# Block-sparse attention and a GELU feed-forward on one core: where the second batch's V is asked for, where GpSimd's copies stand, and how the last product is laid out

## The chip, the cores and the metric

The kernel runs on one core of one Trainium2 chip. The metric is the device time of one execution in microseconds (us); the figure for a kernel is the median of several runs. Engines are named as in the profile: PE (TensorE, matrix products, with PEld for its weight loads), DVE (VectorE), ACT (ScalarE), POOL (GpSimd) and SP (SyncE). Each works through its own list of instructions in order and waits at an instruction until what it needs is there.

## The reference

Attention over 4 batches, 8 heads, 768 positions and 64 numbers a head, in blocks of 32 positions. A query block sees its neighbours, the first and the last block and three sampled ones; the first and the last query block see everything. A feed-forward layer with exact GELU follows, on 3072 tokens.

```python
scores = scale * np.matmul(q, k.transpose(0, 1, 3, 2))
mask = np.abs(blk_i - blk_j) <= window
mask = mask | (blk_i == 0) | (blk_j == 0) | (blk_i == n_blocks - 1) | (blk_j == n_blocks - 1)
for qb in range(n_blocks):
    for kb in sampled_blocks[qb]:
        mask[qb * block:(qb + 1) * block, kb * block:(kb + 1) * block] = True
attn = softmax(np.where(mask, scores, -1e9))      # shortened
x = matmul(attn, v), heads side by side           # 3072 x 512
h = x @ w_in                                      # 512 x 2048
out = (0.5 * h * (1.0 + erf(h * inv_sqrt2))) @ w_out
```

## The kernel before, in words

The 24 tiles of 128 tokens ("quads") are cut into nine **units**: three for batch 0 (one, two and three quads) and two for each further batch (three quads each). Unit numbers run from 0 to 8. A unit goes through attention, then FFN1 (the product with `w_in` and GELU, into the buffer `g`), then FFN2 (the product with `w_out`). The order of instructions on each engine is the order in which the code is written. The loop at the end of the kernel takes unit n: it issues FFN1 of n (`ffn1_step`, eight steps with a GELU each), then attention of unit n+1, into which FFN2 of unit n is strewn as **pieces**. A piece is one matrix product `op` of 128x512; 16 of them make one quad, so a unit has 16, 32 or 48. After the sixteenth, ACT copies the result out of the accumulator (`os`), and SP stores it. There is one accumulator bank for `op`, so the next quad's first piece waits for that copy.

`attention(unit, filler, quota, tail)` goes round by round: PE's scores (`sc`), DVE's maxima (`nm`), ACT's exponentials (`pp`), DVE's transposes (`pT`, `ptd`), PE's products with V (`av`), DVE's division (`den`, `rec`, `xh`), PE's output transposes (`tx`) and ACT's copy into `xT`, which FFN1 reads. `quota` says how many pieces stand in each round, the first number belonging to the round before the first exponentials; `tail` says how many stand ahead of the last `av` group and how many ahead of the last output transposes. What is left over is written behind those transposes.

A round of one unit is "dense" (first and last query block, all keys) or sparse (up to two query blocks). Units 0, 3, 5 and 7 have four dense rounds. I call the transitions into units 3, 5 and 7 **fresh**, since a new batch begins there: its K and Q heads are turned during FFN1 of units 2, 4 and 6. The transitions into units 4, 6 and 8 are **plain**.

Sampled blocks: `gather` copies the keys and values of the sampled blocks of K|V (`kv`, two buffers, one for even and one for odd batches) into `gb`, one copy a block, by DVE or, for the last four query blocks of unit 1, by POOL. The DVE copies for a fresh unit (33 in one go) stand in the second FFN1 step and read the V of that batch. V is loaded by POOL's DMA queue, eight loads a batch, one a head (`load_v`). `hold_loads` puts a one-element copy of `g` ahead of loads on POOL, so that they go out only after a given GELU. The queue is shared with `kn`, `qn` (the next batch's K and Q), `w_in` and `w_out`.

The last unit's FFN2 has no attention beside it.

Of the kernel before, what the change touches and what calls it, by code (L numbers as in the profile page):

```python
# [9 lines left out]
F32 = mybir.dt.float32  # L10
# [9 lines left out]
def kernel(  # L20
# [11 lines left out]
    P = 128  # L32
# [402 lines left out]

    def ffn2_pieces(n):
        for t, quad in enumerate(units[n].quads):
            op = psO.tile([P, D_MODEL], F32, name="op")
            for m in range(KOUT):
                nc.tensor.matmul(op, lhsT=g[:, m, t * P:(t + 1) * P], rhs=w_out_sb[:, m, :],  # L440
                                 start=(m == 0), stop=(m == KOUT - 1))
                if m != KOUT - 1:
                    yield
            os = opool.tile([P, D_MODEL], F32, name="os")
            nc.scalar.copy(os, op)  # L445
            row = units[n].b * S + quad * P
            nc.sync.dma_start(out=out[row:row + P, :], in_=os)
            yield

# [64 lines left out]
    for part in range(2):  # L514
# [3 lines left out]
    gather(units[1], J0[7:], others, KC, BW, nc.gpsimd)  # L518
    ones(1)
    attention(units[0], iter(()), [0] * 7, (0, 0), 5,  # L520
              {4: [lambda: gather(units[0], units[0].js, known, KC, BW)],
               5: [lambda: nc.scalar.copy(kvs[0][:, :, 0:KC], k0)]})

    QUOTAS = {0: ([0, 2, 4, 4, 2], (2, 2)), 1: ([4, 4, 4, 4, 3, 3, 1], (2, 7))}
    for n, unit in enumerate(units):
# [4 lines left out]
        if nxt is not None and not fresh:  # L530
# [4 lines left out]
            elif n == 1:  # L535
                known |= block_numbers(J1[:6], DVE)
                gather(nxt, J1[:4], known)
                hooks[-1] = [lambda u=nxt: gather(u, J1[4:6], known)]
# [6 lines left out]
        for s in range(KOUT // 2):  # L545
            ffn1_step(n, 2 * s)
            if s == 0:
                if n > 0 and not fresh and b + 1 < B:
                    hold_loads(0)
                    for hs in HALVES:  # L550
                        load_kq(kn, k, b + 1, hs)
                    for hs in HALVES:
                        load_kq(qn, q, b + 1, hs)
                if fresh and (b == 0 or b + 2 < B):
                    hold_loads(0)
                    if b == 0:
                        for h in range(H):
                            load_v(1, h)
                    if b + 2 < B:
                        for h in range(H):  # L560
                            load_v(b + 2, h)
# [18 lines left out]
        if nxt is None:  # L580
            for _ in filler:
                pass
        elif n in QUOTAS:
            attention(nxt, filler, *QUOTAS[n], hooks=hooks)
        elif fresh:
            attention(nxt, filler, [4] * 8 + [1, 1, 0], (3, 11))
        else:
            attention(nxt, filler, [6, 5, 5, 5, 5, 6, 2], (3, 11))
# [30 lines left out]
```

## Time and profile before

| | |
|---|---|
| median of 3 runs | 342.42 us (341.29 to 343.58) |
| the profiled execution | 344.02 us, of which the span of the trace is 342.2 |
| PE matmul / weight load busy | 272.3 us (80%) / 155.3 us (45%) |
| DVE busy | 222.0 us (65%) |
| ACT busy | 218.6 us (64%) |
| POOL busy | 51.6 us (15%) |
| chain that ended last, shares of the span | PE 50%, DVE 17%, ACT 15%, DMA 7%, issue 6%, POOL 3% |

Busy shares are means over the whole span. The chain follows the work that ended last back through what released it; "issue" there is time in which an engine waited for nothing that the profile shows. The time between span and run (1.8 us) lies outside the trace.

### The profile page before, as it was taken

How to read it: one execution, taken by the hardware profiler on the slowest of the kernel's cores; microseconds unless marked ns; L12 is line 12 of the kernel's file. 1: busy time of each engine (PE TensorE's matmuls, PEld its weight loads, DVE VectorE, ACT ScalarE, POOL GpSimd, SP SyncE). 2: the span in 40 equal slices, each digit the busy share in tenths (PEclk: the TensorE clock that was granted, in tenths of full speed). 3: DMA queues.
4: the chain of work that ended last, by engine and by line, in shares of the span. 5: the costliest groups of instructions: out<-in, count | busy, mean ns of one | idle time of the engine just before them, and what ended most of it. 6: DMA issues, size and time to landing. Idle time of an engine off the chain costs nothing.

```text
span 342.2 us, 12767 instructions
## 1 busy us (share of the span) xinstructions
PE 272.3 (80%) x5608; PEld 155.3 (45%) x5608; DVE 222.0 (65%) x553; ACT 218.6 (64%) x377; POOL 51.6 (15%) x98
## 2 busy tenths in 40 slices
PE   1753877867991876989899878988898878997994
PEld 1522735534650353535554445545553445454541
DVE  6598666794619795758298887485498877582000
ACT  8675486865482684588367883795378765884621
POOL 8674001100760000300060001200000000000000
PEclk9999999989997899999999999999999999999999
DMA  7999900910999000571099001911000000001001
GB/s 117 134 141 206 178 2 34 179 41 4 86 80 53 33 34 4 100 117 63 35 75 21 33 34 35 173 46 35 33 1 33 33 6 33 1 34 62 3 31 63
DMA packets 39193, 20.74 MB, mean 61 GB/s; under 512 B 25825, under 2 KB 36066, under 8 KB 39138
## 3 DMA queue, kind: packets, MB, share of 16 engines
q0 software_dynamic: 35680, 13.63, 62.9%
q1 hardware_dynamic: 3458, 6.29, 4.8%
q8 instruction: 44, 0.72, 1.0%
q14 instruction: 11, 0.09, 0.1%
HBM read 27.26 MB, written 6.29 MB: 98 GB/s over the span
## 4 chain that ended last, share of the span: by engine, by line
PE 50%; DVE 17%; ACT 15%; DMA 7%; issue 6%; POOL 3%; DVEq 1%; ACTq 0%; POOLq 0%
PE hp L432 22%; PE op L440 14%; ACT pp L324 8%; PE av L387 7%; DVE nm L312 5%; DMA kv<-in_v_dram 4%; DVE pT L341 3%; DMA w_in_sb<-in_moe_w_in_dram 3%; PE sc L287 3%; DVE gb L251 3%; ACT L351 2%; ACT os L445 2%; DVE xh L404 2%; POOL kv L107 2%; ACT g L434 2%
## 5 line engine op out<-in xcount | busy, mean ns | idle before, releaser
L324 ACT ACTIVATE pp<-sc,nm 128x256 bf16<-128x256 f32 (+1 forms) x192 | 91.1, 592 | 21.1 <-DVE nm L315 10.5
L440 PE MATMUL op<-w_out_sb,g 128*128 128x512 bf16 x384 | 97.4, 385 | 5.3 <-ACT os L445 3.3
L432 PE MATMUL hp<-xT,w_in_sb 128*128 128x384 bf16 (+2 forms) x576 | 90.6, 316 | 7.7 <-ACT xT L419 7.7
L434 ACT ACTIVATE g<-hp 128x768 bf16<-128x768 f32 (+2 forms) x72 | 53.3, 740 | 46.1 <-PE hp L432 46.0
L432 PEld LDWEIGHTS <-w_in_sb 128*128 128x128 bf16 x576 | 54.8, 102 | 36.5 <-issue 8.8
L312 DVE TENSOR_REDUCE nm<-sc 128x4 f32<-128x1024 f32 (+1 forms) x48 | 53.1, 1108 | 14.8 <-PE sc L287 14.7
L251 DVE COPY gb<-kv 128x388 bf16 (+1 forms) x252 | 49.6, 277 | 16.0 <-issue 7.4
L440 PEld LDWEIGHTS <-g 128*128 128x128 bf16 x384 | 33.1, 98 | 47.3 <-issue 17.0
L387 PE MATMUL av<-kv,pT 64*32 64x130 bf16 x1760 | 33.4, 229 | 13.6 <-DVE xh L404 7.7
L387 PEld LDWEIGHTS <-pT 64*32 64x32 bf16 x2816 | 28.8, 94 | 23.6 <-DVE xh L404 11.5
L341 DVE STREAM_TRANSPOSE pT<-pp 128x512 f32<-128x512 f32 (+1 forms) x48 | 31.5, 657 | 6.9 <-ACT pp L324 6.8
L287 PEld LDWEIGHTS <-qT 64*32 64x32 bf16 x832 | 10.6, 90 | 50.8 <-issue 41.2
L445 ACT COPY os<-op 128x512 f32<-128x512 f32 x24 | 14.1, 587 | 28.5 <-PE op L440 28.1
L287 PE MATMUL sc<-gb,qT 64*32 64x256 bf16 x704 | 19.6, 283 | 15.9 <-ACT pp L324 15.8
L124 POOL COPY mark<-g 1x1 bf16<-1x1 bf16 x5 | 2.1, 418 | 154.0 <-ACT g L434 154.0
L107 POOL DMA_DIRECT2D kv<-in_v_dram x32 | 23.4, 737 | 4.9 <-DMA kv<-in_v_dram 2.2
L419 ACT COPY xT<-tx 128x512 bf16<-128x512 bf16 (+1 forms) x24 | 13.5, 562 | 16.4 <-PE tx L414 16.4
L387 PE MATMUL av<-gb,pT 64*32 64x130 bf16 x1056 | 20.9, 230 | 2.0 <-issue 2.0
L351 ACT ACT_TABLE_LOAD x17 | 21.8, 1283 | 0.3
L400 DVE TENSOR_SCALAR den<-av 128x8 f32<-128x8 f32 (+2 forms) x28 | 4.3, 155 | 23.6 <-PE av L387 23.1
L404 DVE TENSOR_TENSOR xh<-av,rec 128x512 bf16<-128x512 f32 (+2 forms) x28 | 18.3, 652 | 1.0
L315 DVE TENSOR_REDUCE nm<-sc 128x1 f32<-128x768 f32 x16 | 15.2, 955 | 3.2 <-PE sc L287 3.2
(58 smaller groups left out, 194.3 us busy)
## 6 DMA issues: line engine op xcount, KB each, us to landing
out_dram<-os SPq DMA_DIRECT2D x24, 256.0 KB, 2.0
kn<-in_k_dram POOLq DMA_DIRECT2D x8, 384.0 KB, 5.4
qn<-in_q_dram POOLq DMA_DIRECT2D x8, 384.0 KB, 8.0
kv<-in_v_dram POOLq DMA_DIRECT2D x32, 96.0 KB, 7.7
w_in_sb<-in_moe_w_in_dram POOLq DMA_DIRECT2D x4, 512.0 KB, 12.9
w_out_sb<-in_moe_w_out_dram POOLq DMA_DIRECT2D x2, 1024.0 KB, 20.6
raw<-in_sampled_blocks_dram SPq DMA_DIRECT2D x1, 0.6 KB
```

The source lines that it names most:

```text
L107: nc.gpsimd.dma_start(out=kvs[b % 2][32 * hh:32 * hh + 32, 0:NB, c0:c0 + D], in_=v[b, h].rearrange("(n p) d -> p n d", p=BL))
L251: (engine or nc.vector).tensor_copy(sampled(unit.place[j], r)[:, None, c0:c1], src[:, bass.ds(at[j][r], 1), :])
L287: nc.tensor.matmul(o, lhsT=qT[rows, pr, BL * j:BL * j + BL], rhs=rhs(rows, pr), start=True, stop=True)
L312: nc.vector.tensor_reduce(out=nm[:, 0:2 * n].rearrange("p (g j) -> p g j", g=2), in_=A4[:, :, 0:n, :], op=ALU.max, axis=AX.X, negate=True)
L324: nc.scalar.activation(dst.rearrange("p (c k e) -> p c e k", e=2, k=BL), src.rearrange("p (c e k) -> p c e k", e=2, k=BL), AF.Exp, bias=bias)
L341: nc.vector.transpose(pt[:, 0:w].bitcast(F32), pp[:, 0:w].bitcast(F32))
L351: nc.scalar.activation(junk, zero[0:1, 0:1], func)
L387: nc.tensor.matmul(av[32 * s:32 * s + 32, h, V2 * G:V2 * G + V2], lhsT=pv[rows, c // 2, :, c % 2], rhs=src[rows], start=(c == 0), stop=(c ...
L404: nc.vector.tensor_tensor(xh[rows, :, 0:m * D].rearrange("p h (x d) -> p h x d", d=D), a[:, :, :, 0:D], rec[rows, :, 0:m, None].to_broadca ...
L432: nc.tensor.matmul(hp[:, i, 0:T], lhsT=w_in_sb[:, ki, (m + i) * P:(m + i + 1) * P], rhs=xTs[n % 2][:, ki, 0:T], start=(ki == 0), stop=(ki ...
L434: nc.scalar.activation(g[:, m:m + 2, 0:T], hp[:, :, 0:T], AF.Gelu)
L440: nc.tensor.matmul(op, lhsT=g[:, m, t * P:(t + 1) * P], rhs=w_out_sb[:, m, :], start=(m == 0), stop=(m == KOUT - 1))
```

## The change

There are five edits. V of batch 1 is asked for in the first step of unit 0's FFN1 instead of unit 2's, behind its own `hold_loads(0)`. POOL's twelve value copies for unit 1 (and the ones that complete `kv` 1) stand behind DVE's value copies for unit 0, held by a one-element copy from the block that DVE writes last. In FFN1 of unit 1, DVE makes all eighteen first copies for unit 2 ahead of attention, where six stood behind the first maxima. The numbers of pieces in each round and tail are others: more in the early rounds, fewer ahead of the last transposes, two or three behind them. The last unit's FFN2 goes to four accumulator areas, its last quad in two halves of 256 columns.

```diff
+    def last_output(n):
+        jobs = [(t, quad, slice(0, D_MODEL)) for t, quad in enumerate(units[n].quads)]
+        t, quad, cols = jobs.pop()
+        jobs += [(t, quad, slice(D_MODEL * i // 2, D_MODEL * (i + 1) // 2)) for i in range(2)]
+        two = psV.tile([P, 2, D_MODEL], F32, name="av", tag="V")
+        banks = [psO.tile([P, D_MODEL], F32, name="op"), two[:, 0, :], two[:, 1, :],
+                 psT.tile([P, D_MODEL], F32, name="op", tag="T")]
+        for (t, quad, cols), bank in zip(jobs, banks):
+            op = bank[:, 0:cols.stop - cols.start]
+            for m in range(KOUT):
+                nc.tensor.matmul(op, lhsT=g[:, m, t * P:(t + 1) * P], rhs=w_out_sb[:, m, cols],
+                                 start=(m == 0), stop=(m == KOUT - 1))
+            store(n, quad, cols, op)
...
-    gather(units[1], J0[7:], others, KC, BW, nc.gpsimd)
-    ones(1)
+    def second_values():
+        nc.gpsimd.tensor_copy(mark, sampled(units[0].place[units[0].js[-1]], NR - 1)[0:1, BW - 1:BW])
+        gather(units[1], J0[7:], others, KC, BW, nc.gpsimd)
+        ones(1)
...
-               5: [lambda: nc.scalar.copy(kvs[0][:, :, 0:KC], k0)]})
-    QUOTAS = {0: ([0, 2, 4, 4, 2], (2, 2)), 1: ([4, 4, 4, 4, 3, 3, 1], (2, 7))}
+               5: [lambda: nc.scalar.copy(kvs[0][:, :, 0:KC], k0), second_values]})
+    QUOTAS = {0: ([0, 2, 4, 4, 1], (1, 2)), 1: ([6, 5, 5, 4, 3, 2, 2], (1, 2))}
...
-                gather(nxt, J1[:4], known)
-                hooks[-1] = [lambda u=nxt: gather(u, J1[4:6], known)]
+                gather(nxt, J1[:6], known)
...
+                if n == 0:
+                    hold_loads(0)
+                    for h in range(H):
+                        load_v(1, h)
...
-                if fresh and (b == 0 or b + 2 < B):
+                if fresh and b + 2 < B:
                     hold_loads(0)
-                    if b == 0:
-                        for h in range(H):
-                            load_v(1, h)
...
-            for _ in filler:
-                pass
+            last_output(n)
...
-            attention(nxt, filler, [4] * 8 + [1, 1, 0], (3, 11))
+            attention(nxt, filler, [5, 5, 6, 4, 4, 4, 4, 2, 2, 2, 0], (2, 5))
-            attention(nxt, filler, [6, 5, 5, 5, 5, 6, 2], (3, 11))
+            attention(nxt, filler, [8, 8, 5, 5, 6, 2, 2], (3, 6))
```

How POOL's list changes in the loop, as a difference from before (-) to now (+); `kv_86` and `kv_87` are the buffers of the even and the odd batches, and `mark` is the one-element copy that holds the loads.

```order
 L129 MEMSET kv_87 32x24x2 x4
 L124 COPY mark<-g 1x1
+L107 DMA kv_87<-in_v_dram 32x24x64 x8
+L124 COPY mark<-g 1x1
 L101 DMA kn<-in_k_dram 96x4x512 x2
 L101 DMA qn<-in_q_dram 96x4x512 x2
 L124 COPY mark<-g 1x1
-L107 DMA kv_87<-in_v_dram 32x24x64 x8
 L107 DMA kv_86<-in_v_dram 32x24x64 x8
```

The eight loads of batch 1's V moved ahead of K and Q of that batch, so that only batch 2's eight are left where sixteen stood.

ACT's list in the fresh transition from unit 2 to unit 3, from the table load for exponentials on; the 128x12x2x32 form of `pp` is a dense round, four of the other form are a sparse one.

```order
 L351 ACTIVATE junk<-zero 1x1
-L324 ACTIVATE pp<-sc,nm 128x12x2x32 x3
-L445 COPY os<-op 128x512
-L324 ACTIVATE pp<-sc,nm 128x12x2x32
-L324 ACTIVATE pp<-sc,nm 128x4x2x32 x10
-L445 COPY os<-op 128x512
+L324 ACTIVATE pp<-sc,nm 128x12x2x32 x2
+L439 COPY os<-op 128x512
+L324 ACTIVATE pp<-sc,nm 128x12x2x32 x2
+L324 ACTIVATE pp<-sc,nm 128x4x2x32 x6
+L439 COPY os<-op 128x512
+L324 ACTIVATE pp<-sc,nm 128x4x2x32 x4
```

The first two copies `os` moved ahead of one dense and of one sparse group of exponentials.

ACT's list at the end of the same transition, where FFN1 of unit 3 begins with the first `g`.

```order
-L419 COPY xT_95<-tx 128x4x128
-L445 COPY os<-op 128x512
-L419 COPY xT_95<-tx 128x4x128
+L419 COPY xT_95<-tx 128x4x128 x2
+L439 COPY os<-op 128x512
 L434 ACTIVATE g<-hp 128x768 x8
```

The third `os` moved behind the last copy into `xT`.

## Rows read from the trace of the kernel before

**Rows 1.** Chain that ended last: start, us, what. FFN1 of units 2 to 7.

```profile
85.60 1.47 PE hp L432 x8
...
137.06 10.57 PE hp L432 x64
...
168.42 1.46 PE hp L432 x8
...
209.79 10.57 PE hp L432 x64
...
241.75 1.46 PE hp L432 x8
...
283.89 10.57 PE hp L432 x64
```

**Rows 2.** Timeline of DVE, 101 to 110 us: start, us, what, idle before.

```profile
102.22 5.93 DVE L251 COPY gb<-kv 128x388 bf16 x33 [6.85 <-DMA kv<-in_v_dram]
108.06 1.82 DVE L315 TENSOR_REDUCE nm<-sc 128x1 f32<-128x768 f32 x2
```

**Rows 3.** The same chain, two stretches in unit 3's attention.

```profile
127.55 1.96 issue
...
131.51 1.45 issue
```

**Rows 4.** Windows from the start into each of these stretches; (x) counts instructions.

```profile
0.00:128.50 128.50, 87.64 (x2010) 54.27 (x2010) 90.28 (x222) 83.90 (x140) 38.70 (x79) 0.96 1.30 88
0.00:132.50 132.50, 89.64 (x2138) 55.60 (x2138) 91.50 (x223) 86.06 (x143) 38.70 (x79) 0.96 1.26 85
```

**Rows 5.** Timeline, 24 to 36 us, copies of POOL, DVE and ACT.

```profile
24.28 4.22 POOL L251 COPY gb<-kv 128x260 bf16 x12
24.92 5.71 DVE L251 COPY gb<-kv 128x260 bf16 x12
...
30.71 2.86 ACT L522 COPY kv<-qT 128x3200 bf16<-128x3200 bf16 x1 [3.89 <-DVE gb L251]
...
35.66 0.61 DVE L235 COPY gb<-qT 128x768 bf16<-128x768 bf16 x2
```

**Rows 6.** The chain again: DVE's value copies of unit 0.

```profile
28.50 2.13 DVE gb L251 x11
```

**Rows 7.** All instructions on the tile w_out_sb.

```profile
L118 POOL DMA_DIRECT2D w_out_sb<-in_moe_w_out_dram x2: 876/881/886, 18.9 to 20.2; - x2
...
DMA to landing us min/median/max: 18.7/20.6/22.5
```

**Rows 8.** Timeline, 280 to 284 us: end of unit 7's attention.

```profile
280.19 2.54 PE L440 MATMUL op<-w_out_sb,g 128*128 128x512 bf16 x11
...
280.51 0.69 DVE L404 TENSOR_TENSOR xh<-av,rec 128x512 bf16<-128x512 f32 x1
...
282.56 0.39 PE L414 MATMUL tx<-identity,xh 128*128 128x128 bf16 x4
...
282.76 0.59 ACT L445 COPY os<-op 128x512 f32<-128x512 f32 x1 [1.79 <-PE op L440]
...
283.24 0.59 ACT L419 COPY xT<-tx 128x512 bf16<-128x512 bf16 x1
```

**Rows 9.** Timeline of ACT, 188 to 190.5 us: dense rounds of unit 5.

```profile
188.25 1.11 ACT L324 ACTIVATE pp<-sc,nm 128x768 bf16<-128x768 f32 x1 [0.65 <-DVE nm L315]
189.62 0.59 ACT L445 COPY os<-op 128x512 f32<-128x512 f32 x1 [0.26 <-PE op L440]
```

**Rows 10.** Timeline, unit 2's first round on DVE.

```profile
65.44 1.10 DVE L251 COPY gb<-kv 128x388 bf16 x6
```

**Rows 11.** Timeline: FFN1 of unit 1, and the last product.

```profile
56.74 7.15 PE L432 MATMUL hp<-xT,w_in_sb 128*128 128x256 bf16 x64 [0.67 <-ACT xT L419]
...
334.48 3.61 PE L440 MATMUL op<-w_out_sb,g 128*128 128x512 bf16 x16 [0.72 <-ACT os L445]
...
338.18 0.59 ACT L445 COPY os<-op 128x512 f32<-128x512 f32 x1 [3.74 <-PE op L440]
```

More of the change, by code (lines that the diff above doesn't have):

```diff
@@ L434, in ffn1_step, with store @@
         nc.scalar.activation(g[:, m:m + 2, 0:T], hp[:, :, 0:T], AF.Gelu)
+    def store(n, quad, cols, op):
+        w = cols.stop - cols.start
+        os = opool.tile([P, w], F32, name="os")
+        nc.scalar.copy(os, op)
+        row = units[n].b * S + quad * P
+        nc.sync.dma_start(out=out[row:row + P, cols], in_=os)
     def ffn2_pieces(n):
@@ L443, in ffn2_pieces @@
                     yield
[L444 to L447, printed above, removed]
+            store(n, quad, slice(0, D_MODEL), op)
             yield
+    def last_output(n):
[11 more added lines that the diff above has]
+            store(n, quad, cols, op)
     def attention(unit, filler, quota, tail, held=0, hooks=None):
@@ L553 @@
                         load_kq(qn, q, b + 1, hs)
-                if fresh and (b == 0 or b + 2 < B):
+                if fresh and b + 2 < B:
                     hold_loads(0)
-                    if b == 0:
-                        for h in range(H):
-                            load_v(1, h)
-                    if b + 2 < B:
-                        for h in range(H):
-                            load_v(b + 2, h)
+                    for h in range(H):
+                        load_v(b + 2, h)
                 if fresh:
```

## The prediction

> **What bounds the kernel now.** I began with the chain that ended last, to find the places where FFN1 starts: they cut the run into stages that can be compared with each other [rows 1]. From one FFN1 start to the next, a stage with a fresh transition takes 137.06 - 85.60 = 51.46 us the first time, 209.79 - 168.42 = 41.37 the second and 283.89 - 241.75 = 42.14 the third. All three do the same work, so some 9.3 to 10.1 us of the first are waits. The timeline shows the largest: DVE stands 6.85 us until V of batch 1 has landed, then makes its 33 copies in 5.93 us, and only at 108.06 comes to the first maxima [rows 2]. Late in the same stage PE stands 1.96 and 1.45 us for nothing that the profile names [rows 3]. The counts up to these stops are 2010 and 2138 matmuls with as many weight loads [rows 4]: 128 pairs, 256 instructions apart. PE goes on at 129.51 and 132.96, 3.45 us apart. I read this as the supply of PE's instructions, in portions of 256, of which one takes some 3.45 us to come; a stretch of short products with V uses them up faster. Elsewhere the kernel is bound by a relay of PE, DVE and ACT inside attention, by PE in FFN1, and at the end by PE and ACT taking turns.
>
> **V of batch 1.** Nothing is added or removed in work, eight loads move from behind 85.60 to about 36 us (an estimate: the first GELU of unit 0, moved as below). Sixteen loads in a row landed in at most 102.22 - 85.60 = 16.6 us [rows 1, 2], so eight asked for at 36 are there long before DVE wants them; that wait goes whole. What is late next is known, since the second and third fresh stages have no such wait: the stage becomes 41.37 us [rows 1], if PE's instructions come in time. The first fresh stage begins at the same instruction count as before, since each stage keeps its number of pieces, so the borders between portions still fall into its products with V. Going through the new order with the durations of the second fresh stage and 3.45 us for a portion, I find PE at three borders early, by 1.0, 1.6 and 0.5 us; about 1.0 of this replaces waits that the stage has anyway, so I add 2.1. Gain: 51.46 - (41.37 + 2.1) = 8.0, and 0.1 from the pieces (below): 8.1 us. The ends: 10.1 if no portion is late, and 51.46 - 41.37 - 1.96 - 1.45 = 6.7 if both stops stay as they are.
>
> The moved loads pass POOL's queue. They stand behind `w_out`, whose second half is asked for at 20.2 and lands by 20.2 + 22.5 = 42.7 [rows 7]. On POOL only K and Q of batch 1 are queued behind them, held until the first GELU of unit 1's FFN1, which starts at 56.74 today [rows 11]. I cost the move at nothing, because they are queued after `w_out`; what it would cost if they shared the engines with it is a rival below.
>
> *A rule against this reading of PE's stops.* The Trainium skill ("Runtime: NRT & Kernel Launch", section "Instruction fetch mechanics") says that instructions come in blocks of 256, which agrees with rows 4, and that crossing from one to the next is mostly hidden, which rows 3 contradict at two places. By that rule the sum would keep the whole 10.1.
>
> **GpSimd's value copies.** POOL's twelve copies run from 24.28 to 28.50, DVE's twelve start at 24.92 [rows 5], and eleven of them run from 28.50 to 30.63 [rows 6]. So DVE's first copy sat through POOL's, and a copy takes 2.13 / 11 = 0.19. Alone the twelve end at 24.92 + 2.3 = 27.2 instead of 30.63: 3.4 us earlier, and unit 0's transposes, products, division and FFN1 follow DVE there. POOL's copies now wait for DVE and then for ACT's 2.86 us copy of the keys [rows 5], which starts near 27.2: they run from about 30.1 to 34.3. DVE reaches its fixed copies for unit 1 at 35.66 - 3.4 = 32.3 [rows 5] and would stand until 34.3, 2.0 us, if POOL again held it to the end. Those copies have a lead over unit 1's first scores of about the same size, as FFN1 of unit 0 lies between. I take 0.2 as the cost, and 0 to 2.0 as its bounds. Gain 3.2, between 1.4 and 3.5.
>
> *What the skill says of this.* "SBUF — State Buffer", section "SBUF: two separate sides", in the Trainium skill, calls the port that VectorE and GpSimd share a lock for one whole instruction. Rows 5 and 6 show more: DVE waited through all that was left of twelve instructions. By the page DVE would get in between two of them, and the 0.2 would be gone.
>
> **Unit 2's first round.** Six copies of 1.10 us stand between its first and second maxima [rows 10]. They move into FFN1 of unit 1, where DVE waits for scores. The exponentials follow the maxima there, so about 0.9 comes back. Here the third `os` no longer stands ahead of the last copy into `xT`, and PE has fewer pieces ahead of the last transposes, worth 0.7, against three pieces more ahead of the last product with V (0.2 each). Sum 1.3 us, between 0.5 and 1.8.
>
> **The pieces.** At the end of a stage `xh` is ready at 280.51 + 0.69 = 281.20, but eleven pieces last until 282.73, so the transposes run at 282.56; then `os` delays `xT` to 283.24 [rows 8]. With five pieces of 0.23 us ahead, PE is free at 281.35, `tx` runs then and `xT` starts at about 281.9: 1.3 us earlier. The three pieces left run beside the 0.59 us of `xT`, which nearly hides them. So a full transition returns 1.3. Against that, pieces moved ahead delay attention. In a fresh transition 5 + 5 + 6 pieces fill the first quad two groups of exponentials in, and its `os` stands ahead of the third, where before `os` came at 189.62, behind the exponentials of 188.25 [rows 9]. ACT must now wait for the longer run of pieces (to 188.5, as I walk it) and copy for 0.59: the third exponentials start at 189.1 or so, 0.9 later. Each round hands that on, since the accumulator of the scores is freed by the exponentials, and three more pieces, 0.7 us, stand in the rounds. Followed to the end, the last product with V ends 1.2 us later, of the gain of 1.3 there remains 0.1. In a plain transition two pieces more stand in the rounds and `os` moves one group earlier; followed through, that costs 0.3, and PE's stop at a portion border becomes 0.1 shorter, which leaves 1.1. Sum: three plain transitions 3.3, the two fresh ones not yet counted 0.2. Bounds: fresh from a loss of 1.0 to a gain of 1.3, plain from 0.1 to 1.3. The transition into unit 1 has 16 pieces, and its last transposes already wait for `xh`: nothing.
>
> **The last product.** Two times PE waits for `os`, 0.72 us each or nearly [rows 11]: 1.4, since each quad now has its own bank. Two halves cost no more than one whole: with 256 columns 64 products took 7.15, so 32 take 3.58, against 3.61 for 16 full ones. The last copy, 0.59, has half the columns, about 0.2 to 0.3 less, and its store half the bytes, 0 to 0.3. Sum 1.7, between 1.4 and 2.0.
>
> **Sum.** 8.1 + 3.2 + 1.3 + 3.3 + 0.2 + 1.7 = 17.8 us. The profiled execution took 344.02, 342.2 of it the span, so its like would take 326.2; against the median of 342.42, which is 1.6 lower, it is **324.6 us**.
>
> **The rivals.**
> *Instructions come in time.* The first fresh stage becomes like its twins, 41.37 us. For it: the second stage passes the same kind of products without a stop. Against it: rows 3 and 4, and that the borders lie where they lay. Then the gain is 19.8 to 20: 322.5 us.
> *The moved pieces eat what they free.* If every early piece delays the scores, and `os` the exponentials, by its whole length, a fresh transition loses 1.0 and a plain one gains nothing: 17.8 - 3 x 1.1 - 3.3 = 11.2, so 331.2 us. For it: ACT's idle time ahead of `os` in rows 9 is only 0.26 us. Against it: PE waits for exponentials in the same rounds, so part of a piece is free.
> *The loads hold up w_out.* Eight loads could share the engines with the second half of `w_out` and delay it by half of the 16.6 us above, 8.3; FFN2 of unit 0 wants it, by my walk, some 3 us after it lands today. Loss 5: 329.6 us. Against it: the loads are asked for 15 us later.
> *Slower than before: portions late everywhere.* Eight transitions hold products with V, and in the fresh ones two pieces instead of three stand between the last two groups of them. If each transition had two stops like rows 3, 3.41 us, of which 2.1 is already counted once, that would cost 8 x 3.41 - 2.1 = 25.2: 349.8 us. It outweighs the 17.8 from (17.8 + 2.1) / 8 = 2.5 us per transition on. Against it: the plain transitions keep five pieces there, and the fresh ones gain two ahead of the last group but one.
>
> **How the numbers follow.** Chances: the forecast 0.54 (322.9 to 328), instructions in time 0.24, moved pieces 0.14, loads against `w_out` 0.03, slower 0.02; and 0.03 that several losses together leave less than 1%, which is about what a measurement of this kernel tells from no change. The bounds of single terms do not add up to more than 4 us either way. A range of 320.5 to 330.5 leaves out the slow half of the piece rival and the last three, some 0.15. Faster by over 1%: 0.95; within 1%: 0.03; slower: 0.02.
>
> **What the profile after would show.** No wait of DVE for V ahead of unit 3, and first maxima some 7 us sooner behind the start of unit 2's FFN1 than the 108.06 - 85.60 = 22.5 of now. DVE's value copies of unit 0 done in 2.3 us. Transposes of the last group within 1.5 us of the last product with V, and `xT` straight behind. In fresh transitions an `os` ahead of the third exponentials and a last product with V about 1.2 us later than now. PE without a gap in the last product. The prediction is wrong if the first fresh stage still takes over 45 us, if fresh stages grow, or if FFN1 of unit 0 doesn't start some 3 us earlier.

## The result

The changed kernel takes 330.07 us (median of four runs, 329.59 to 330.38), the kernel before 343.00 in the same comparison: ratio 0.9625, interval 0.9579 to 0.9672. The profiled execution took 329.59 us with a span of 327.81, against 342.17 before: 14.36 us less, where the terms of the sum gave 17.8. In the timed runs the medians are 12.93 apart.

Stage by stage: "first" is the start of the first FFN1 in the timeline, "0" to "7" run from the first matmul of one unit's FFN1 to that of the next, "8" from the last FFN1 to the end. Stages 2, 4 and 6 hold the fresh transitions; 3, 5 and 7, the plain ones, are added up. All rows are of the one profiled execution of each kernel; the last column is the median of its timed runs, in us like all the others. The runs e1 to e12 are the experiments below.

| | first | 0 | 1 | 2 | 4 | 6 | 3+5+7 | 8 | span | median |
|---|---|---|---|---|---|---|---|---|---|---|
| before | 37.08 | 19.66 | 28.87 | 51.46 | 41.37 | 42.14 | 94.90 | 26.70 | 342.17 | 343.00 |
| after | 33.61 | 21.29 | 28.25 | 43.45 | 43.25 | 41.69 | 90.87 | 25.41 | 327.81 | 330.07 |
| e1 V late | 33.63 | 19.36 | 28.54 | 52.44 | 43.00 | 42.00 | 90.79 | 25.33 | 335.07 | 335.34 |
| e2 old pieces | 33.60 | 21.06 | 29.03 | 43.69 | 41.36 | 41.85 | 95.19 | 25.40 | 331.18 | 337.18 |
| e3 mixed pieces | 33.61 | 21.03 | 28.21 | 43.87 | 41.37 | 42.25 | 91.55 | 25.40 | 327.29 | 330.24 |
| e4 borders moved | 37.33 | 19.65 | 28.15 | 41.32 | 41.32 | 43.37 | 92.66 | 25.40 | 329.20 | 330.20 |
| e5 GpSimd first | 35.54 | 20.16 | 28.22 | 42.57 | 41.32 | 41.32 | 91.27 | 25.94 | 326.34 | 329.06 |
| e6 even fresh | 33.66 | 23.11 | 29.49 | 42.11 | 40.26 | 40.15 | 91.14 | 25.40 | 325.32 | 326.49 |
| e7 even, padded | 33.20 | 22.44 | 28.21 | 41.25 | 39.82 | 41.30 | 90.77 | 25.39 | 322.37 | 323.77 |
| e8 V alone | 37.13 | 20.22 | 28.66 | 43.09 | 41.36 | 41.84 | 94.63 | 26.70 | 333.64 | 335.75 |
| e9 V one FFN1 later | 33.61 | 19.64 | 30.77 | 42.13 | 41.30 | 41.31 | 91.25 | 25.32 | 325.33 | 327.09 |
| e10 = e6 and e9 | 33.29 | 20.05 | 29.94 | 42.57 | 39.79 | 39.89 | 90.23 | 25.32 | 321.09 | 322.97 |
| e11 = e10, padded | 33.61 | 19.93 | 29.67 | 40.70 | 39.82 | 39.82 | 90.82 | 25.32 | 319.70 | 321.08 |
| e12 changed, again | 33.21 | 21.11 | 28.44 | 45.01 | 41.32 | 41.96 | 91.08 | 25.40 | 327.53 | 329.32 |

The chain that ended last after the change, at the places of [rows 1 and 3]. Where the record of a first product is missing, it names an FFN1 up to 0.2 us late.

```profile
33.61 3.01 PE hp L432 x32
...
50.32 1.68 issue
...
54.90 7.18 PE hp L432 x64
...
83.15 1.46 PE hp L432 x8
...
118.47 1.19 issue
...
126.60 10.56 PE hp L432 x64
...
156.87 1.38 PE hp L432 x8
...
200.19 10.40 PE hp L432 x64
```

One of the two stops of PE in stage 2 (the lines "issue") is left, and there is a new one of 1.68 us in stage 0, where the chain before had none.

DVE's timeline in FFN1 of unit 2 answers [rows 2]:

```profile
92.74 5.71 DVE L251 COPY gb<-kv 128x388 bf16 x33
98.52 0.96 DVE L315 TENSOR_REDUCE nm<-sc 128x1 f32<-128x768 f32 x1
```

The wait for V is gone. The first maxima come 98.52 - 83.15 = 15.4 us behind the start of FFN1, 7.1 sooner.

The timeline from 24 to 36 us answers [rows 5 and 6]:

```profile
24.91 1.98 DVE L251 COPY gb<-kv 128x260 bf16 x12
...
26.93 2.86 ACT L545 COPY kv<-qT 128x3200 bf16<-128x3200 bf16 x1
...
29.85 4.33 POOL L251 COPY gb<-kv 128x260 bf16 x12 [2.71 <-ACT kv L545]
...
32.18 1.65 DVE L235 COPY gb<-qT 128x768 bf16<-128x768 bf16 x6
```

DVE's twelve copies take 1.98 us instead of 5.71. Its fixed copies for unit 1 run in 1.65 us in the middle of GpSimd's burst: the block of up to 2.0 us that the prediction kept as a bound did not come.

The end of unit 7's attention, timeline of PE, ACT and DVE, against [rows 8]:

```profile
269.92 0.69 DVE L404 TENSOR_TENSOR xh<-av,rec 128x512 bf16<-128x512 f32 x1
...
270.67 0.39 PE L414 MATMUL tx<-identity,xh 128*128 128x128 bf16 x4
...
271.10 0.58 ACT L419 COPY xT<-tx 128x512 bf16<-128x512 bf16 x1 [0.72 <-PE tx L414]
...
271.74 0.49 PE L432 MATMUL hp<-xT,w_in_sb 128*128 128x384 bf16 x2
```

The transposes follow `xh` at once and `xT` follows them, without the `os` ahead of it.

The last product, timeline of PE and ACT, against [rows 11]:

```profile
316.26 3.62 PE L465 MATMUL av<-w_out_sb,g 128*128 128x512 bf16 x16
...
320.59 1.91 PE L465 MATMUL av<-w_out_sb,g 128*128 128x256 bf16 x16 [0.72 <-ACT os L439]
...
324.33 0.37 ACT L439 COPY os<-op 128x256 f32<-128x256 f32 x1 [1.38 <-PE op L465]
```

One of the two waits for `os` is still there.

### The profile page after: what moved, and what is told of

It is laid out like the page before. It is cut to its first block, busy times and chain, and to the rows that moved or that the text cites. A ratio compares the mean times of both kernels' runs of the same rounds, so it can differ in the third digit from the quotient of the medians.

```text
span 327.8 us, 12763 instructions
## 1 busy us (share of the span) xinstructions
PE 269.1 (82%) x5582; PEld 155.8 (48%) x5624; DVE 220.1 (67%) x553; ACT 218.9 (67%) x378; POOL 52.6 (16%) x100
## 4 chain that ended last, share of the span: by engine, by line
PE 58%; DVE 15%; ACT 13%; issue 6%; DMA 5%; POOL 1%; DVEq 1%; ACTq 0%; POOLq 0%
PE hp L432 25%; PE op L447 13%; ACT pp L324 8%; PE av L387 6%; DVE pT L341 4%; DVE nm L312 4%; PE sc L287 3%; DMA w_in_sb<-in_moe_w_in_dram 3%; DVE xh L404 3%; DMA kv<-in_v_dram 2%; DVE kv L204 2%; PE av L465 2%; PE pt L193 2%; PE op L465 2%; ACT L351 2%
## 5 line engine op out<-in xcount | busy, mean ns | idle before, releaser
L432 PE MATMUL hp<-xT,w_in_sb 128*128 128x384 bf16 (+2 forms) x576 | 89.3, 312 | 1.2 <-ACT xT L419 0.9
L447 PE MATMUL op<-w_out_sb,g 128*128 128x512 bf16 x295 | 80.3, 390 | 9.4 <-issue 4.8
L432 PEld LDWEIGHTS <-w_in_sb 128*128 128x128 bf16 x576 | 53.4, 100 | 32.1 <-issue 3.2
L251 DVE COPY gb<-kv 128x388 bf16 (+1 forms) x252 | 46.0, 262 | 10.2 <-issue 8.6
L447 PEld LDWEIGHTS <-g 128*128 128x128 bf16 x336 | 28.5, 100 | 37.5 <-issue 15.5
L387 PE MATMUL av<-kv,pT 64*32 64x130 bf16 x1760 | 35.0, 229 | 12.8 <-DVE xh L404 5.4
L439 ACT COPY os<-op 128x512 f32<-128x512 f32 (+1 forms) x23 | 13.3, 576 | 19.7 <-PE op L447 15.4
L124 POOL COPY mark<-g 1x1 bf16<-1x1 bf16 x6 | 3.6, 594 | 137.1 <-ACT g L434 137.0
L400 DVE TENSOR_SCALAR den<-av 128x8 f32<-128x8 f32 (+2 forms) x28 | 4.4, 155 | 21.2 <-PE av L387 20.7
```

The costliest lines, as they stand in the source:

```text
L251: (engine or nc.vector).tensor_copy(sampled(unit.place[j], r)[:, None, c0:c1], src[:, bass.ds(at[j][r], 1), :])
L387: nc.tensor.matmul(av[32 * s:32 * s + 32, h, V2 * G:V2 * G + V2], lhsT=pv[rows, c // 2, :, c % 2], rhs=src[rows], start=(c == 0), stop=(c ...
L432: nc.tensor.matmul(hp[:, i, 0:T], lhsT=w_in_sb[:, ki, (m + i) * P:(m + i + 1) * P], rhs=xTs[n % 2][:, ki, 0:T], start=(ki == 0), stop=(ki ...
```

## The experiments

Three readings were to be told apart: what the early V does outside of stage 2, whether stage 4 lost its 1.9 us to the moved pieces or to the clock, and what the other parts are worth by themselves.

### V of batch 1: e1, e8, e9 and the repeat e12

**e1_v_late** undoes this part alone, **e8_v_alone** makes it alone in the kernel before.

```diff
-                if n == 0:
-                    hold_loads(0)
-                    for h in range(H):
-                        load_v(1, h)
...
-                if fresh and b + 2 < B:
+                if fresh and (b == 0 or b + 2 < B):
```

> The changed kernel with V of batch 1 asked for in unit 2's FFN1 again, all else as changed. Stage n is the time from the start of unit n's FFN1 to the next one's. If the early V is worth what the traces suggest, stage 2 grows from 43.5 to about 51.5 and the median from 330.1 to 338. On stage 0, which grew from 19.7 to 21.3 us: by the theory that a portion of PE's instructions came late (between the last two groups of products with V there are fewer pieces), it stays at 21.3 with a PE stop near 1.7 us; by the rival, that the V loads in flight held up PE's instructions or w_out, it falls to 19.7 and the stop is gone.

Measured: 335.34 us, 0.9753 of before (0.9673 to 0.9832). Stage 2 goes back to 52.44 and stage 0 falls to 19.36. So, between these two profiles, V early is worth 9.0 us in stage 2 and costs 1.9 in stage 0. Not all of either is V's: the granted clock is 0.50 for 13.7 us of stage 2 in e1 and for 3.4 in the changed kernel, and for 3.4 us of stage 0 in the changed kernel and not in e1. By the medians the part is worth 5.3 us, or 6.0 against the repeat e12; the profiled execution of e1 is its slowest.

> The kernel before with one part of the change alone: V of batch 1 asked for in unit 0's FFN1. Theory (the part is worth 9 us in stage 2, of which a late portion in stage 0 takes some back when V's loads are in flight): stage 2 falls from 51.5 to 43 to 44, stage 0 stays at 19.7 or grows by up to 2, since the later FFN1 start puts the loads behind more of w_out, all else within 0.5; time 6.5 to 9 us below the kernel before. Rival (the 9 us hang on the other parts too, the new pieces in that stage above all): stage 2 falls by under 7, and the time by under 5.5.

Measured: 335.75 us, 0.9791 (0.9731 to 0.9852), 7.0 below before. Stage 2 is 43.09, so the gain does not hang on the pieces. Stage 0 grows only by 0.56 here. Its first FFN1 starts at 37.13, 3.5 us later than in the changed kernel, and the chain has no stop in stage 0.

**What the stop in stage 0 is.** In the changed kernel, timelines of POOL and PE:

```profile
35.86 5.08 POOL L107 DMA_DIRECT2D kv<-in_v_dram  x7
44.45 0.71 POOL L107 DMA_DIRECT2D kv<-in_v_dram  x1 [3.51 <-DMA w_out_sb<-in_moe_w_out_dram]
...
49.89 0.43 PE L387 MATMUL av<-kv,pT 64*32 64x130 bf16 x26
52.01 0.30 PE L387 MATMUL av<-kv,pT 64*32 64x130 bf16 x14 [1.68 <-issue]
```

V's eighth load waits for `w_out`, and V's packets fill the DMA engines from about 42 us, when `w_out` is almost in. The windows of the changed kernel (time, busy time and count of PE, weight loads, DVE, ACT, POOL; granted clock, DMA share, GB/s; the share passes 1 where the times of packets overlap):

```profile
46.00:48.00 2.00, 1.84 (x100) 1.08 (x99) 1.32 (x4) 1.49 (x4) 0.00 (x0) 0.97 4.31 92
48.00:50.00 2.00, 0.93 (x71) 0.64 (x70) 1.38 (x3) 1.73 (x3) 0.00 (x0) 1.00 3.61 78
50.00:52.00 2.00, 0.32 (x39) 0.19 (x24) 0.00 (x0) 0.00 (x0) 0.00 (x0) 1.00 0.44 6
```

They do so up to about 50 us, under the products with V of unit 1, which use up instructions fastest (some 100 products with their weight loads in the first of these windows, against 20 and 21 in the two ahead of it). **e9_v_in_ffn1_1** asks for V one FFN1 later.

```diff
-                if n == 0:
+                if n == 1:
                     hold_loads(0)
                     for h in range(H):
                         load_v(1, h)
```

> The changed kernel, with V of batch 1 asked for in the first step of unit 1's FFN1 (ahead of K and Q of that batch) instead of unit 0's. Theory (the stop of stage 0 is a portion of instructions that is late because V's packets fill the DMA engines from 42 to 50 us, while the products with V use portions up): with no load in flight there, the stop at 50.3 goes and stage 0 takes 19.2 to 19.9 instead of 21.3, the first FFN1 stays at 33.5, stage 2 stays within 0.7 of 43.5, stage 1 within 0.7 of 28.3; time 1.5 to 2.5 us below the changed kernel, 327 to 328.5. Rival (the border lies badly there, loads or not): stage 0 stays above 20.8 and the time within 1 us of 330. Second rival (loads slow any portion that they meet): stage 0 falls, but V, K and Q now fill the engines from 55 to 76 us and stage 1 grows by 1 us or more, so that the time stays within 1 us of 330.

Measured: 327.09 us, 0.9542 (0.9479 to 0.9605). The same windows in e9:

```profile
46.00:48.00 2.00, 1.84 (x100) 1.07 (x99) 1.17 (x3) 1.54 (x5) 0.00 (x0) 0.88 0.02 4
48.00:50.00 2.00, 0.93 (x50) 0.46 (x49) 1.52 (x4) 1.71 (x3) 0.00 (x0) 1.00 0.03 8
50.00:52.00 2.00, 1.59 (x108) 1.09 (x95) 0.94 (x3) 0.48 (x1) 0.00 (x0) 1.00 0.03 8
```

Up to 48 us PE does the same, with and without V's packets; then it stops in one and runs on in the other. Order and borders of PE's list are the same in both. The view of the DMA queues from 47 to 52 us shows the packets that bring PE's instructions; changed kernel first, then e9 (packets, MB, share of 16 engines):

```profile
q8 instruction: 1, 0.02, 1.9%
```

```profile
q8 instruction: 2, 0.03, 2.4%
```

One packet of instructions takes 1.9% x 16 x 5 = 1.5 us beside V's packets, 2.4% x 16 x 5 / 2 = 0.96 without. Over all traces this holds with bounds: in the nine runs with V in unit 0's FFN1, the packet that meets V's takes 1.54 to 1.98 us, and the 398 packets behind 20 us that meet no other traffic take 0.88 to 1.48. In the changed kernel the packet is in flight from 48.91 to 50.45 us and PE goes on at 52.01; in e9 it is in flight from 48.00 to 48.93. The stops of other places hang on packets too: all 27 of over 1.0 us that the chains of the 14 traces show behind the first FFN1 end 1.2 to 1.8 us after such a packet has landed. So the theory holds: stage 0 falls to 19.64, although the clock is at 0.50 there for 3.4 us from 43.1, as in the changed kernel from 42.7. With the clock alike in both, the loads cost 21.29 - 19.64 = 1.65 us. But the second rival's outcome came too. Stage 1 grows by 2.5, to 30.77, with loads in flight up to some 75 us (to 68 in the changed kernel), 0.50 in two stretches, from 70.4 and from 80.6, and two stops in the chain of e9:

```profile
74.99 1.22 issue
...
79.22 0.99 issue
```

The second lies behind the loads, so how much of the 2.5 is theirs stays open. The sum of stages 0 and 1 is 50.41 in e9 and 49.54 in the changed kernel. What the time gained, 3 us, comes in the profiles from stages 2 and 4, which have the same code in both; the next run shows how far such stages differ by themselves.

**e12_again** is the changed kernel itself, with no edit.

> The changed kernel once more, for a second profile of it. If the half clock at the end of stage 4 (196.1 to 199.6) belongs to the new order of pieces there, it is there again and stage 4 takes 43.0 to 43.4. If it falls where it will, stage 4 takes 41.2 to 41.5, as in e5_pool_first and e9_v_in_ffn1_1, which have the same pieces there, and the span is about 326. The stop near 50.3 in stage 0 should be there either way (0.8 to 3 us, stage 0 20.8 to 23.2), since V's packets and the portion meet in every run; if it is not, that reading falls.

Measured: 329.32 us, 0.96 (0.9516 to 0.9685). The stop in stage 0 is there again, at 49.69 for 1.44 us. Stage 4 takes 41.32. Windows at its end, changed kernel first, then e12:

```profile
197.00:198.00 1.00, 1.00 (x3) 0.38 (x3) 1.00 (x3) 0.33 (x1) 0.00 (x0) 0.50 0.00 0
198.00:199.00 1.00, 1.00 (x6) 0.52 (x5) 1.00 (x2) 0.00 (x0) 0.00 (x0) 0.50 0.00 0
```

```profile
197.00:198.00 1.00, 1.00 (x9) 0.53 (x8) 0.91 (x3) 0.59 (x1) 0.00 (x0) 1.00 0.00 0
198.00:199.00 1.00, 1.00 (x9) 0.53 (x8) 1.00 (x3) 0.36 (x1) 0.00 (x0) 1.00 0.00 0
```

The granted clock is 0.50 in the one, 1.2 GHz, and 1.00 in the other, 2.4 GHz, in the same program at the same place. So the 1.9 us of stage 4 are not the pieces' own price. But stage 2 takes 45.01 in e12, with a stop of 2.03 us and the clock at 0.50 for 6.8 us from 119.7 on.

### GpSimd's copies: e5

```diff
-    def second_values():
-        nc.gpsimd.tensor_copy(mark, sampled(units[0].place[units[0].js[-1]], NR - 1)[0:1, BW - 1:BW])
-        gather(units[1], J0[7:], others, KC, BW, nc.gpsimd)
-        ones(1)
+    gather(units[1], J0[7:], others, KC, BW, nc.gpsimd)
+    ones(1)
```

> The changed kernel with one part undone: GpSimd's twelve value copies for unit 1 stand ahead of DVE's copies for unit 0 again. Theory (DVE's first copy sits through the GpSimd copies that are under way): DVE's twelve copies take 5 to 6 us instead of 1.98, the first FFN1 starts at 36.8 to 37.3 instead of 33.5, all stages behind it stay within 0.5 us of the changed kernel, and the time is 3 to 4 us above it, 333 to 334 us. Rival (the earlier start comes from something else in the new order of DVE or ACT, the port being free between two instructions): the first FFN1 stays within 1 us of 33.5 and the time within 1 us of the changed kernel. A third outcome would be that the later start moves the V loads away from the late portion in stage 0, so that stage 0 falls from 21.3 to 19.7 and only about 2 us are lost.

Measured: 329.06 us, 0.9602 (0.9541 to 0.9663): no slower than the changed kernel. Timelines of DVE and POOL in e5, then the durations of the copies from `kv` in the kernel before and in e5 (min/median/max in ns, from all instructions on `gb`):

```profile
24.91 3.99 DVE L251 COPY gb<-kv 128x260 bf16 x12
...
25.30 4.22 POOL L251 COPY gb<-kv 128x260 bf16 x12
```

```profile
L251 DVE COPY gb<-kv x252: 209/254/3912, 24.9 to 291.9; 128x388 bf16 x120, 128x260 bf16 x6
```

```profile
L251 DVE COPY gb<-kv x252: 241/252/519, 24.9 to 279.5; 128x388 bf16 x120, 128x260 bf16 x6
```

Here DVE began 0.39 us ahead of GpSimd, and its copies were slowed to 0.33 us each; no copy took over 0.52. In the kernel before, GpSimd began 0.64 ahead [rows 5], and one DVE copy took 3.91; in e8, which has the same order, GpSimd began 0.57 ahead and one took 3.97. So the first FFN1 starts 1.9 us later and not 3.5, and the third outcome came on top: stage 0 is 1.1 shorter, since the products with V run that much later against V's packets. The changed order is worth 3.75 us when V is late (first FFN1 and stage 0 add up to 52.99 in e1, which also has unit 0's new numbers, and to 56.74 before), but beside the early V, by the same sum, 55.70 - 54.90 = 0.8 against the changed kernel's first profile and 1.4 against its second (54.32). In the whole time nothing of it is left: 329.06 is below the medians 330.07 and 329.32 of the changed kernel.

### The pieces: e2, e3 and e6

**e2_old_pieces** has the kernel before's numbers in all transitions, **e3_mixed_pieces** in the first and the fresh ones alone (of the diff, unit 0's list and the first pair).

```diff
-    QUOTAS = {0: ([0, 2, 4, 4, 1], (1, 2)), 1: ([6, 5, 5, 4, 3, 2, 2], (1, 2))}
+    QUOTAS = {0: ([0, 2, 4, 4, 2], (2, 2)), 1: ([4, 4, 4, 4, 3, 3, 1], (2, 7))}
-            attention(nxt, filler, [5, 5, 6, 4, 4, 4, 4, 2, 2, 2, 0], (2, 5))
+            attention(nxt, filler, [4] * 8 + [1, 1, 0], (3, 11))
-            attention(nxt, filler, [8, 8, 5, 5, 6, 2, 2], (3, 6))
+            attention(nxt, filler, [6, 5, 5, 5, 5, 6, 2], (3, 11))
```

> The changed kernel with the numbers of pieces of before in all transitions (and so no pieces behind the last output transposes). If the thinner end of attention is what lengthened stages 0 and 4, stage 0 falls from 21.3 to 19.7 and stage 4 from 43.3 to 41.4, and the plain stages 3, 5 and 7 grow by 0.9 to 1.9 each (30.2, 30.0, 30.7 to 31.4, 32.0, 31.6): about -3.5 and +4, so 330 to 331. By the rival, that the moved pieces are a gain everywhere and the longer stages come from elsewhere (loads, clock of that one run), all transitions grow by about 1.2 and the median is 336 or more.

Measured: 337.18 us, 0.9831 (0.9758 to 0.9904). The profiled execution took 332.95; the other four took 336.63 to 337.87, at a mean granted clock of 0.962 to 0.978 against 0.987, and no trace shows where their 4 to 5 us lie. In the profile the plain stages grow by 4.3, stage 1 by 0.8, stage 4 is 1.9 shorter, and stage 0 stays at 21.06. So the theory's figure for the time (330 to 331) is missed, and the rival's, 336 or more, came, though not by its stages: stage 4 did not grow.

> The changed kernel with the pieces of before in stage 0 and in the fresh stages 2, 4 and 6, and the new ones in stage 1 and the plain stages. By the theory of the thin end: stage 0 at 19.7, stage 4 at 41.4, stage 6 at 42.1, stage 2 at 43 to 45 (its instruction portions come late in either order), the plain ones unchanged: median 326.5 to 328.5. By the rival that the new numbers are a gain everywhere: 334 or more.

Measured: 330.24 us, 0.9623 (0.9522 to 0.9724), the same as the changed kernel within the interval. The theory's 326.5 to 328.5 is missed: stage 0 is 1.3 above its figure. Between the profiles of e2 and e3, the new numbers give 3.6 in the plain stages; the medians are 6.9 apart. In stage 4 both take 41.36 to 41.37, against 41.30 to 41.32 with the new numbers at full clock (e4, e5, e9, e12): the moved pieces return 0.05 there. Stage 0 keeps its stop in both, so that does not come from the pieces.

**e6_even_fresh** spreads the pieces of the fresh transitions evenly again and keeps five behind the last `av`. Its first unit's numbers are those of the changed kernel; the words in its expectation that they are those of before are wrong (they are so in e7).

```diff
-            attention(nxt, filler, [5, 5, 6, 4, 4, 4, 4, 2, 2, 2, 0], (2, 5))
+            attention(nxt, filler, [4] * 8 + [2, 2, 1], (3, 5))
```

> The changed kernel with another share of pieces in the fresh transitions: four in each of the first eight rounds, then 2, 2, 1, tail 3 and 5 (first unit's quota as in the kernel before). Theory (the 5 + 5 + 6 ahead of the third exponentials put os in ACT's way and take pieces from the rounds where PE then idles, which is what the 1.9 us in stage 4 and the half clock at its end are; the few pieces behind the last transposes are right): stages 4 and 6 take 39.8 to 41.0 instead of 43.2 and 41.7, no half clock in stage 4, time 325 to 328 us. Rival (the half clock at the end of stage 4 is a matter of the clock's history and not of the pieces): stage 4 stays above 42.5 with a half-clock stretch in it, and the time stays within 1.5 us of 330.

Measured: 326.49 us, 0.9508 (0.9444 to 0.9571). Stages 4 and 6 take 40.26 and 40.15, 1.1 less than either order. ACT's timeline in stage 4, e12 (the changed kernel) first, then e6:

```profile
178.19 0.59 ACT L439 COPY os<-op 128x512 f32<-128x512 f32 x1 [1.03 <-PE op L447]
178.67 2.15 ACT L324 ACTIVATE pp<-sc,nm 128x768 bf16<-128x768 f32 x2
```

```profile
178.21 1.12 ACT L324 ACTIVATE pp<-sc,nm 128x768 bf16<-128x768 f32 x1 [0.64 <-DVE nm L315]
179.58 0.59 ACT L439 COPY os<-op 128x512 f32<-128x512 f32 x1 [0.25 <-PE op L447]
```

Their FFN1 began at 157.96 and 158.39: the third exponentials start 20.71 us behind it with `os` ahead, 19.82 with `os` behind, and 19.83 in the kernel before [rows 9]. So the order of the changed kernel loses 0.9 us there and wins it back at the end; e6 has the gain alone. The rival's number for stage 4 falls, though e12 shows it right on the 1.9 us: the gain here is against the stage at full clock. Stage 0 has the stop again, 2.98 us with 0.50 behind it (23.11).

### The borders between portions: e4, e7, e10 and e11

**e4_shift_64** issues unit 0's score products twice, with the same result, which is 64 pairs more ahead of all later work.

```diff
+        twice = 2 if unit is units[0] else 1
-            for i, j in enumerate(rnd[1]):
+            for i, j in twice * list(enumerate(rnd[1])):
-            for c0, c1 in ((0, 512), (512, 768)):
+            for c0, c1 in twice * ((0, 512), (512, 768)):
```

> The changed kernel with every score product of unit 0 made twice (same result, 64 matmuls and weight loads more), which moves every border of 256 instructions by half a portion against the program. Unit 0 becomes 1 to 4 us longer. By the theory of portions: the stop of 1.7 us in stage 0 is gone (its border falls 64 pairs earlier in the program), that of 1.2 us in stage 2 is gone or under 0.5, and one of 0.5 to 2 us appears in stage 6, which had none, since its borders now lie where stage 2's lay. By the rival, that the stops belong to these places of the program (a transfer, a semaphore), they stay at the same instructions.

Measured, in two runs: 330.20 us, 0.9614 (0.9516 to 0.9712). The stops of stages 0 and 2 are gone, and stage 2 takes 41.32, as long as its twin stage 4 in the same run. Others came: the chain has 2.14 us ahead of the first FFN1, 2.08 in stage 3 and 1.55 in stage 5. The one expected in stage 6 is there with 0.58, and the clock is at 0.50 for 3.4 us from 268.8: stage 6 takes 43.37, 2.0 more than its twin. The first FFN1 starts 3.7 us later by the doubled products and that stop, so by e5 and e8 stage 0 says nothing on the border.

**e7_even_fresh_pad** is e6 with the first unit's old numbers and products of one column that nobody reads: for each unit, the round and how many.

```diff
+    PAD = {1: (0, 64), 3: (4, 48), 5: (4, 16), 7: (4, 32)}
+            if it == PAD.get(units.index(unit), (None, 0))[0]:
+                pad(PAD[units.index(unit)][1])
```

> As e6_even_fresh, with added products of one column into a tile that nobody reads, which only move the borders between instruction portions: 64 in the transition of stage 0, and 48, 16 and 32 more in the fresh transitions of stages 2, 4 and 6. Theory (PE's stops come where a border of 256 instructions falls into a stretch of short products): the stops in stages 0 and 2 go, stage 0 takes 19.4 to 20.2 and stage 2 40.5 to 42.0, against 21.0 and 43.5 without; no stop over 1 us in stages 4 and 6; time 1.5 to 4 us under e6_even_fresh. Rival (the stop in stage 0 comes from the loads in flight alone, wherever the border lies): stage 0 stays at 21 or grows by the added products, some 1 to 2 us, and the time is not below e6_even_fresh.

Measured: 323.77 us, 0.9408 (0.9332 to 0.9484). Stage 0 stays at 22.44, with a stop of 2.44 at 49.03: there the rival holds, a border 64 pairs further on still falls under V's packets. In stage 2 a stop of 1.03 us is left and it takes 41.25. In stage 6, for which no stop of over 1 us was expected, the chain has 1.33 at 263.52, and the 1.1 us that e6 had won there are lost again (41.30): a shift moves all later borders too.

**e10_v_even** puts e6 and e9 together, **e11_v_even_pad** adds `PAD = {2: (0, 64), 3: (4, 48), 5: (4, 16)}`.

> Both changes of e6_even_fresh and e9_v_in_ffn1_1 together. If both are worth what the stages say: stage 0 19.2 to 19.9 (23.1 in e6_even_fresh), stage 1 28.2, stage 2 41.5 to 42.5, stages 4 and 6 40.0 to 40.6, time 321 to 323.5 us. If the stop only moves, to stage 1 or 2: 325 to 327 us.

> As e10_v_even, with added products of one column into a tile that nobody reads: 64 in the transition of stage 1, 48 of stage 2 and 16 of stage 4, which move the borders between portions as far as e7_even_fresh_pad did in stage 2 and bring them back for stages 4 and 6. If the stops in stage 2 depend on where the borders lie: stage 2 0.6 to 1.2 us under e10_v_even, the added products in stage 1 cost 0 to 0.7, all else within 0.4; time 0 to 1 us below e10_v_even. If not, the time is 0.5 to 1.5 us above it.

Measured: 322.97 us, 0.9415 (0.9369 to 0.9461), and 321.08, 0.9345 (0.9294 to 0.9397). Both keep about what the single runs had in stages 0, 4 and 6; stage 1 misses the expected 28.2, as it did in e9. Windows of e10 in stage 2, behind its stop of 2.46 us at 117.11:

```profile
118.00:119.00 1.00, 0.00 (x0) 0.00 (x0) 0.00 (x0) 0.98 (x3) 0.00 (x0) 1.00 0.00 0
119.00:120.00 1.00, 0.26 (x1) 0.13 (x2) 0.13 (x1) 1.00 (x1) 0.00 (x0) 0.60 0.00 0
120.00:121.00 1.00, 0.83 (x2) 0.29 (x2) 0.93 (x4) 0.25 (x2) 0.00 (x0) 0.50 0.00 0
```

PE stands, and as it goes on the clock is at its lower level, 0.50. With the borders 112 pairs further on in e11, the longest stop of the stage is 0.71, the clock stays at 1.00 and stage 2 takes 40.70 instead of 42.57. The 64 products added in stage 1 take 0.63 us in a row, beside waits: the stage is not longer (29.67, 29.94 in e10). That the borders matter does not rest on this pair alone: in the three runs that move them, stage 2 takes 40.70 to 41.32 without a stretch at 0.50 (e4, e7, e11); in the nine others with V early it takes 42.1 to 45.0. e11 is the fastest of all.

## Why the prediction was right, and where its sum was off

The forecast was 324.6 us; 330.07 lies in the range, 0.4 us from its slow end, and outside the band of 322.9 to 328 to which the forecast gave 0.54. Of the 5.5 us between, 3.4 lie in the terms below. The other 2.1 come from the step to the median: it took off 1.6, by which the profiled execution was slower than the median before, and after the change the profiled one was 0.5 faster than the median. By stages, forecast and measured gain in the two profiled executions:

| term | forecast | measured |
|---|---|---|
| V early, stage 2 | 8.1 | 8.0 |
| V early, elsewhere (stage 0) | 0 | -1.6 |
| GpSimd's copies (first FFN1) | 3.2 | 3.5 |
| unit 2's first round, stage 1 | 1.3 | 0.6 |
| plain transitions | 3.3 | 4.0 |
| fresh transitions, stages 4 and 6 | 0.2 | -1.4 |
| last product, stage 8 | 1.7 | 1.3 |
| sum | 17.8 | 14.4 |

**V early** was right in its mechanism: the wait for V went whole, and the stage fell to its twin's time of before plus what late portions leave. That they leave something is shown by e4 and e11, where the stage without a long stop takes 41.32 and 40.70. The size of the rest, 2.1, was luck: it was to come from three late borders, and what came is one stop of 1.19 us and a stretch at the lower clock. With the same borders stage 2 took 42.1 to 45.0. The wait was also more than a wait. Windows of the kernel before, then of the changed one:

```profile
103.00:110.00 7.00, 0.30 (x2) 0.09 (x1) 6.88 (x33) 0.95 (x1) 0.00 (x0) 0.80 3.48 58
110.00:112.00 2.00, 1.80 (x11) 0.57 (x11) 1.50 (x3) 1.10 (x2) 0.00 (x0) 0.50 0.03 2
```

```profile
121.10:126.60 5.50, 4.84 (x144) 3.23 (x145) 3.10 (x7) 1.69 (x4) 0.00 (x0) 0.69 0.01 3
```

PE stood for want of V and of the copies from it, and then ran at 0.50 for 6.8 us in all (107.2 to 114.0); the changed kernel has 3.4 us at 0.50 in this stage, from 121.2. The sum had no term for the clock, and how much of the 8.0 is the clock's is not shown. The Trainium skill ("Runtime: NRT & Kernel Launch", section "Instruction fetch mechanics") calls the crossing of blocks mostly hidden; the stops of up to 2.46 us in this stage decide against it here.

**The step that failed** is "I cost the move at nothing, because they are queued after `w_out`". The queue did keep the loads off `w_out` (it lands by 21.5 + 22.7 = 44.2 us; in e1, without them, by 20.7 + 22.7 = 43.4). It sent them instead, all at once, into the time of the products with V of stage 0, where they slow the packets of PE's own instructions: 1.6 us in the table, 1.65 between e9 and the changed kernel. The prediction had both halves, the price of a portion and the time of the loads, and did not lay one over the other. The rival "the loads hold up `w_out`" looked at the right transfer and the wrong victim. (Its 329.6 us is counted out of the range of 320.5 to 330.5, in which it lies.)

**GpSimd's copies.** Size and place were right, 3.5. The reason is narrower than stated: DVE sits through GpSimd's burst when it comes behind its start (before, e8) and not when it comes first (e5, one run). The lock for one whole instruction, as the Trainium skill has it ("SBUF — State Buffer", section "SBUF: two separate sides"), fits e5, where DVE got in between GpSimd's copies, and not the 3.91 us of the kernel before. The prediction also took the terms as independent; e1 and e5 show that 3.75 us are worth 0.8 to 1.4 beside the early V in the first two stages, and nothing in the whole time. The reading is that an earlier attention meets V's packets: in e4, e5 and e8, whose first FFN1 starts 1.9 to 3.7 us later, PE has no stop in stage 0.

**Unit 2's first round** was forecast from two things. The earlier copies returned nothing: with them and the old numbers stage 1 takes 29.03 (e2), and 28.87 before. The pieces returned 0.6 (28.44 in e12 against 29.03, both with a stretch at 0.50 there).

**Plain transitions** gave 0.9 to 1.9 each in place of 1.1; that the pieces gave it is shown by e2 and e3, why it is more is open.

**Fresh transitions.** The walk was right step by step. In e12, at full clock, the third exponentials come 0.88 us later (forecast 0.9); the last product with V starts 195.73 - 157.96 = 37.77 us behind FFN1, and in the kernel before, at 204.69, 36.27: 1.5 later (forecast 1.2); and the stage is 0.05 shorter (forecast 0.1). The 1.9 us lost in stage 4 of the profile are PE's lower clock, of which the prediction had no term. Whether the new order makes that likelier is open: in stages 4 and 6, the lower clock came in 3 of 12 passes with it (after, e1, e4) and in none of 16 with the old or even order. The prediction named growing fresh stages, and a first one of over 45 us, as signs that it is wrong. Stage 4 did grow in the first profile and stage 2 took 45.01 in e12; neither came in both profiles of the changed kernel.

**The last product.** Four banks removed one wait of 0.72, not two: the third job shares the tile `av` with the second, and waited for that tile's `os`, though its half is another one. The last copy is 0.22 shorter and what follows it about 0.3, as forecast.

The rivals: instructions did not come in time, the pieces did not eat their gain, and the portions were not late everywhere. What came was the forecast with two costs that none of them named.

## What to carry to other kernels

A load that is moved to where nothing waits for it is still not free: look at which engine uses up instructions fastest while its packets are in flight, and lay the loads under long instructions, not under streams of short ones. Once the borders between instruction portions show as stops, they can be moved with a few products that nobody reads (1.9 us between e10 and e11), with a look at the later stages, whose borders move too (e7). And one profile of a kernel is not enough to put a difference of 2 us in one stage down to an edit: the changed kernel's own two differ by 1.9 in stage 4 and 1.6 in stage 2. Last, a gain that ends at a transition should be asked what it cost earlier in the same stage: keeping the old even order and only shortening the tail was worth 1.1 us a stage more than the order that was tried.

## What the hardware showed that I had not expected

- A packet of instructions took 0.88 to 1.48 us where it met no other traffic and 1.54 to 1.98 beside V's many small packets in stage 0. In six of those nine runs PE stopped behind it under products with V, for 1.3 to 3.0 us; in e4, e5 and e8 it came ahead of those products, with PE at 20 or 21 products in 2 us or fewer, and PE did not stop.
- A stop can be paid twice. In e10 and e12 PE stood for 2.46 and 2.03 us, and the granted clock fell to 0.50 before it went on; but in e3 it stood for 2.20 and 1.68 us in the same stage, and the clock stayed at 1.00. The same program fell to 0.50 in stage 4 in one profile and not in the next, so that this stage differs by 1.9 us with the code unchanged.
- DVE's copies of 260 columns came to 0.165 us alone, 0.33 beside GpSimd's burst when DVE began first, and one took 3.9 when GpSimd had begun; six copies of 768 columns from `qT` ran at the same 1.65 us inside that burst as without it (e5, behind it).
